# A linear-attention block with a gated feed-forward layer: the last block's output projection by seven half-size products, and a new order of issue

## The chip, the cores and the metric

The kernel runs on one core of a Trainium2 chip. A core has five engines that run side by side, each through its own queue in order: TensorE (PE, matmuls into the eight PSUM banks), VectorE (DVE), ScalarE (ACT), GpSimd (POOL) and SyncE (SP). Here GpSimd also issues the loads from HBM, and SyncE the stores and the transposes that run as transfers. The metric is the device time of one execution in microseconds (us), lower is better.

## The reference

The first stage is attention with projected keys and values. For each of 8 batches and 8 heads, with a sequence of 1024 and a head size of 64:

```python
k_proj = np.einsum('ks,bhsd->bhkd', E, k)          # 1024 rows -> 64
v_proj = np.einsum('ks,bhsd->bhkd', F, v)
scores = scale * np.matmul(q, k_proj.transpose(0, 1, 3, 2))
scores = scores - np.max(scores, axis=-1, keepdims=True)
attn = np.exp(scores)
attn = attn / (np.sum(attn, axis=-1, keepdims=True) + 1e-09)
attn_out = np.matmul(attn, v_proj)
```

The heads are put side by side, which gives x of 8192 x 512, and the second stage is a gated layer with a hidden width of 1536:

```python
gate = 1.0 / (1.0 + np.exp(-(x @ w_gate)))
val = x @ w_val
out = gate * val @ w_out
```

## The kernel before

Tokens are worked through in 16 blocks of 512, two blocks to a batch. A block goes through the gate and value products, a tanh on ScalarE, the hidden product `hT` on VectorE (1536 x 512, bf16, hidden units on partitions), and the output projection with `w_out` into `ost`, which is stored in four pieces of 256 KB (`store`, L1253). The attention of batch b+2 and b+1 is worked on while the blocks of batch b are multiplied.

*Seven products for eight.* The gate and value products (`seven`, L1108) and the output projections of blocks 1 to 14 (`o_jobs`, L1324) cut both matrices into 2 x 2 quarters and form the result from seven products of quarters, with sums of quarters made ahead by VectorE or GpSimd. For an output projection the quarters of `hT` are tokens by hidden units: `s_sum` (L1206) makes S1 = A21 + A22, S2 = S1 - A11, then, in the place of A21, A11 - A21, and, in the place of A12, A12 - S2 (S4). The sums of the weights are made once, into `wT` (`o_sum`, L1193). One product of quarters is two half-products of six matmuls of 256 columns (`o_product`, L1222). Three PSUM banks take part: a chain of products accumulates in one, ScalarE copies snapshots of it out (`snap`), and VectorE joins them with another bank (`merge`, L1355) or ScalarE copies a quarter out (`leave`, L1348). The product A12 x B21 reads A12 before S4 overwrites it, and the last product, A12 x B22, reads S4.

*Plain.* Blocks 0 and 15 go through `o_plain` (L1264) instead, since `o0p=1` and `o3p=1` in the table `AT` (L30):

```python
if AT[f"o{0 if not blk else 3 if blk == 2 * B - 1 else 2 - blk % 2}p"] > 0:
    return o_plain(blk, pos, step)
```

For block 15 that is three pieces of 128 tokens of 12 matmuls of 512 columns each, and the last piece in two halves of 12 matmuls of 256 columns. Each piece is copied out by ScalarE and stored by itself. In the issue order the piece of tokens 0 to 127 is last.

*The loads.* K and V of one batch come in two halves of 512 KB each (`load_kv`, L561; R is the half), q likewise (`load_q`, L582), all issued by GpSimd in its own order. K's buffer also serves as the place where the attention's result waits to be transposed into x (`turn_x`, L1709), so a half of K can be loaded only when the transposes of two token groups of the batch before have read it. `kv` (L1449) projects K and V in 16 matmuls of 512 columns and waits for all four halves. `transpose_q` (L1435) turns two heads of q at a time, four transfers for a batch, on SyncE's queue; the first waits for its half of q, and all that stands behind it on this queue waits with it. `turn_kd` (L1478) turns the projected K, and the scores (`score_pair`, L1622) wait for it and for q.

*The order.* A planner outside the kernel has written the order down. Each piece of work is a job with a number, in the order in which the code makes the jobs; `ORDER` (L159) lists the numbers in the order in which they are issued, each on its engine, and `PLACES` (L314) the PSUM bank or buffer of each tile that a job uses. A negative number in `ORDER` is a fill: idle matmuls of 256 columns times its size (`busy`, L724), so -2 is one of 512 columns. `Scheduler.run` (L359) reads both:

```python
for s, p in zip(slots, PLACES):
    s.at = p
return [(lambda i=i: fill(-i)) if i < 0 else self.jobs[i].body for i in ORDER]
```

Waits follow from the data (`Plan.add`), through semaphores, and an engine waits in `run` (L121) before the instruction that needs it. The constants of time in `AT` and `FB` set nothing any more, except the switches among them.

The numbers that matter below, for batch 2: 415 and 416 load the halves of K, 417 and 418 those of V, 419 loads the half of q that transposes 421 and 422 need and 420 the other, 421 to 424 are the four transposes of q, 425 is the projection, 428 turns the projected K, 581, 589, 597 and 605 are the scores.

Of the kernel before, what the change touches and what calls it, by code (L numbers as in the profile page):

```python
# [29 lines left out]
    s2=0, s3=0, s4=0, s5=0, s6=0, s7=0, o0p=1, o1p=0, o2p=0, o3p=1, x1=0, x2=0, x3=0, x4=1, g1=0, g2=0, g3=0,  # L30
# [123 lines left out]
class Job:  # L154
# [5 lines left out]
    16, -2, -2, -2, 17, 18, 0, 19, -2, -2, -2, -1, 30, 20, 4, 28, 21, 29, 5, 31, 1, -2, -2, -2, -2, -2, -2, 38,  # L160
    32, 22, 8, 33, 23, 39, 2, 34, 50, 24, 3, 48, 51, 40, 25, 35, -2, 26, 41, 36, 27, 42, 49, 37, -2, -2, -2, -2,
    -2, -2, -2, -1, 58, 52, 59, 68, 53, 43, 60, 61, -2, -1, 54, 69, 6, 55, 62, 44, 70, 46, 7, 75, 45, 47, 56,
    76, 9, 71, 72, 63, 10, 73, 57, -2, -2, 66, 13, 74, 77, -2, -1, 64, 14, 67, 140, 65, 78, 146, 12, 79, 134,
    194, 80, 81, 135, 128, 141, 195, 129, 130, 142, 197, 132, 136, 131, 138, 196, 143, 133, 144, 148, 137, 145,
    11, 84, 82, 188, 85, 147, 83, 149, 139, 15, 86, 104, 87, 102, 201, 105, 92, 152, 93, 103, 150, 88, 199, 164,
    94, 89, 106, 160, 362, 90, 156, 107, 162, 91, 95, 151, 112, 157, 154, 185, 96, 168, 108, 97, 172, 113, 109,
    184, 166, 114, 180, 158, 187, 110, 115, 100, 161, 101, 116, 111, 182, 98, 173, 174, 99, 170, 159, 122, 117,
    169, 175, 123, 163, 124, 200, 118, 120, 119, 181, 121, 171, 198, 125, 183, 218, 126, 234, 127, 186, 219,
    282, 202, 235, 165, 189, 190, 283, 210, 191, 220, 212, 222, 203, 221, 250, 167, 223, 238, 204, 251, 236,
    192, 239, 286, 193, 205, 224, 237, 225, 411, 254, 226, 241, 252, 207, 242, 206, 229, 227, 287, 245, 230,  # L170
    412, 240, 253, 284, 243, 153, 255, 228, 246, 298, 208, 257, 299, 209, 289, 155, 285, 231, 244, 258, 247,
    266, 232, 300, 248, 233, 261, 211, 267, 176, 249, 290, 270, 413, 262, 256, 178, 314, 301, 326, 271, 213,
    259, 273, 328, 272, 414, 274, 177, 315, 217, 329, 275, 302, 316, 260, 268, 216, 179, 263, 317, 327, 293,
    276, 318, 277, 294, 264, 319, 278, 279, 265, 439, 214, 303, 215, 320, 280, 269, 420, 281, 330, 547, 440,
    346, 338, 334, 442, 331, 335, 332, 336, 549, 333, 304, 342, 443, 337, 321, 339, 343, 305, 441, 322, 350,
    445, 306, 347, 323, 344, 340, 324, 348, 341, 351, 349, 309, 345, 307, 325, 363, 288, 352, 364, 354, 310,
    446, 311, 353, 355, 365, 370, 448, 291, 366, 444, 371, 358, 372, 447, 292, 356, 373, 359, 357, 375, 382,
    308, 367, 360, 295, 376, 553, 368, 548, 361, 377, 383, 369, 384, 387, 554, 449, 550, 385, 296, 374, 391,
    379, 555, 565, 388, 378, 380, 297, 381, 562, 389, 312, 386, 563, 552, 313, 394, 399, 564, 566, 392, 450,
    400, 395, 551, 556, 396, 401, 393, 397, 403, 567, 404, 419, 568, 390, 406, 557, 569, 407, 405, 408, 515,  # L180
    402, 431, 398, 467, 516, 531, 561, 451, 432, 517, 532, 433, 434, 571, 518, 533, 452, 572, 409, 534, 455,
    418, 573, 410, 453, 468, 560, 535, 456, 519, 454, 457, 415, 458, 520, 469, 417, 459, 522, 536, 460, 471,
    558, 523, 521, 570, 461, 538, 470, 559, 462, 577, 526, 423, 524, 463, 464, 539, 483, 527, 422, 528, 484,
    542, 489, 472, 543, 421, 485, 465, 474, 537, 529, 475, 424, 487, 416, 540, 473, 488, 478, 435, 578, 490,
    436, 544, 476, 438, 491, 499, 545, 525, 494, 486, 492, 480, 495, 574, 437, 481, 530, 496, 466, 681, 546,
    500, 575, 482, 493, 697, 479, 501, 698, 576, 503, 505, 497, 504, 701, 477, 682, 506, 702, 541, 745, 507,
    683, 502, 685, 508, 510, 686, 425, 778, 684, 511, 746, 509, 498, 777, 512, 426, 780, 687, 513, 688, 427,
    779, 704, 689, 699, 514, 428, 705, 747, 690, 692, 708, 700, 580, 693, 703, 579, 429, 709, 761, 694, 748,
    706, 783, 430, 781, 666, 710, 762, 695, 784, 664, 711, 763, 785, 782, 581, 691, 764, 749, 786, 582, 750,
    585, 787, 696, 583, 765, 791, 790, 752, 712, 584, 597, 586, 753, 789, 589, 792, 766, 590, 587, 768, 593,  # L190
    788, 756, 588, 769, 591, 793, 757, 598, 713, 794, 594, 751, 592, 797, 601, 595, 772, 599, 714, 596, 798,
    602, 600, 715, 754, 603, 717, 773, 716, 620, 617, 604, 758, 718, 618, 621, 707, 729, 622, 767, 799, 619,
    623, 605, 755, 759, 720, 665, 606, 613, 801, 721, 614, 609, 730, 802, 615, 607, 733, 803, 616, 770, 625,
    724, 734, 626, 731, 771, 725, 624, 774, 627, 610, 629, 736, 608, 628, 630, 632, 732, 760, 795, 611, 633,
    796, 775, 634, 612, 737, 644, 735, 635, 800, 637, 719, 631, 740, 638, 645, 636, 722, 639, 917, 738, 640,
    723, 641, 726, 642, 667, 918, 643, 727, 742, 656, 670, 804, 743, 728, 646, 805, 657, 744, 658, 919, 649,
    879, 776, 815, 650, 806, 651, 920, 816, 677, 921, 809, 679, 880, 810, 678, 817, 808, 741, 680, 883, 819,
    884, 653, 647, 885, 820, 654, 886, 818, 659, 822, 648, 887, 881, 652, 823, 888, 821, 882, 669, 890, 655,
    925, 892, 824, 891, 895, 660, 893, 831, 896, 828, 739, 832, 847, 829, 807, 825, 899, 668, 833, 900, 835,
    834, 848, 902, 836, 897, 903, 851, 898, 894, 838, 811, 826, 852, 912, 863, 911, 827, 854, 864, 812, 849,  # L200
    914, 814, 906, 850, 853, 907, 855, 867, 889, 662, 901, 856, 839, 1045, 904, 924, 860, 868, 858, 861, 842,
    663, 913, 870, 1046, 908, 843, 923, 1047, 909, 871, 1049, 1061, 922, 859, 910, 926, 905, 1062, 927, 661,
    1048, 869, 813, 1050, 915, 1063, 830, 874, 862, 1064, 837, 857, 1065, 916, 875, 929, 928, 840, 865, 931,
    866, 844, 872, 932, 873, 1052, 933, 876, 841, 1053, 1051, 845, 1066, 930, 877, 1056, 1141, 1068, 671, 1054,
    1069, 934, 1055, 846, 878, 1067, 672, 1058, 1070, 1109, 673, 1142, 1072, 1059, 1057, 938, 674, 1143, 1060,
    1074, 1146, 1110, 935, 1075, 936, 1073, 1125, 1144, 937, 1111, 1071, 1126, 939, 1145, 1112, 1127, 675, 940,
    1113, 1076, 1147, 676, 944, 942, 1128, 945, 1114, 943, 953, 949, 1148, 946, 1116, 1149, 950, 1129, 1117,
    1150, 947, 1130, 1120, 957, 948, 1132, 954, 951, 1151, 1121, 958, 952, 1156, 1155, 1153, 955, 961, 959, 969,
    1133, 965, 1157, 1152, 956, 962, 1136, 1158, 960, 970, 1077, 1161, 966, 1078, 1162, 963, 941, 967, 1081,
    973, 964, 1079, 971, 1163, 984, 968, 1131, 1080, 1137, 1165, 1082, 985, 974, 981, 986, 996, 1084, 972, 997,  # L210
    982, 989, 998, 1166, 983, 975, 999, 990, 993, 991, 1115, 976, 994, 1167, 987, 1093, 995, 1085, 977, 1118,
    992, 1083, 1094, 1088, 978, 1086, 979, 1001, 1154, 1122, 1000, 1134, 1008, 1095, 1123, 980, 1138, 1009,
    1097, 1002, 1096, 1003, 1159, 988, 1124, 1139, 1160, 1098, 1010, 1090, 1164, 1013, 1011, 1017, 1020, 1100,
    1018, 1091, 1004, 1168, 1101, 1014, 1140, 1169, 1015, 1029, 1019, 1089, 1104, 1027, 1041, 1092, 1005, 1021,
    1243, 1105, 1119, 1099, 1022, 1042, 1179, 1244, 1043, 1044, 1195, 1006, 1180, 1007, 1247, 1102, 1245, 1248,
    1016, 1183, 1170, 1181, 1184, 1023, 1250, 1174, 1182, 1106, 1012, 1196, 1249, 1107, 1246, 1186, 1024, 1197,
    1251, 1199, 1087, 1252, 1259, 1187, 1032, 1108, 1185, 1200, 1256, 1260, 1190, 1257, 1172, 1202, 1191, 1173,
    1135, 1254, 1203, 1211, 1103, 1255, 1261, 1188, 1212, 1206, 1263, 1207, 1281, 1264, 1276, 1213, 1198, 1192,
    1026, 1265, 1193, 1227, 1030, 1175, 1266, 1262, 1215, 1025, 1267, 1409, 1228, 1268, 1270, 1028, 1216, 1282,
# [1655 lines left out]
```

## Time and profile before

| | us |
|---|---|
| median of three executions | 518.62 (518.52, 518.62, 525.71) |
| the profiled execution | 523.59 |
| its span, first to last instruction | 521.6 |
| TensorE busy | 511.5 |
| VectorE busy | 433.9 |
| ScalarE busy | 371.9 |
| GpSimd busy | 171.2 |

A line of the timeline gives the start, the time taken, the engine, the line of the kernel, the operation with its output and inputs, how many instructions are joined in it, and in brackets the idle time before it and what ended that. In the stretches each engine has its busy time with the number of its instructions, and the last three figures are the clock granted to TensorE as a share of full speed, the share of the transfer engines and GB/s. A line of a queue (SPq) spans from the start of its first issue to the end of its last. "To landing" counts from a transfer's issue to its end. L516 is the helper through which all matmuls go, L530 that of ScalarE's copies, L545 that of sums, L1102 a plus, L1171 a hidden product, L557 a load, L1438 a transpose of q, L1481 that of the projected K, L1257 a store; PSUM banks are pF and pA.

### The profile page before, as it was taken

Reading aid. Unit: us, or ns where it says so; the run is one execution under the profiler, and the core shown is the slowest. Engines: PE = TensorE matmul, PEld = TensorE weight load, DVE = VectorE, ACT = ScalarE, POOL = GpSimd, SP = SyncE. Lnnn points to the kernel's source line nnn. Section 1 sums busy time; section 2 is a strip of 40 time slices with the busy share of each in tenths; the row PEclk is TensorE's granted clock in tenths of the full one; section 3 lists DMA queues with packets and bytes.
Section 4 is the critical chain, followed back from the end, with each engine's and each line's share of the span. In section 5 each row is a group of like instructions: output and inputs, shape, how many; then the busy total and the mean of one; then the engine's idle time right before and its main releaser. Section 6 shows DMA issues by size and latency. Waiting matters only on the chain.

```text
span 521.6 us, 12583 instructions
## 1 busy us (share of the span) xinstructions
PE 511.5 (98%) x4954; PEld 419.6 (80%) x4954; DVE 433.9 (83%) x847; ACT 371.9 (71%) x714; POOL 171.2 (33%) x200
## 2 busy tenths in 40 slices
PE   7999999979999999999999999999999999999997
PEld 4556757868898888888888888988898878888884
DVE  5779998496978999789987898989978799849880
ACT  1557866876978687876977778786887679676751
POOL 9894004601343114250263313440153400350020
PEclk9999999998999999999999999999999999999999
DMA  9999979996797536996999899981679923452004
GB/s 154 197 198 207 192 113 161 170 145 143 129 178 129 94 102 123 164 192 131 152 164 206 116 164 173 181 144 21 163 123 186 178 64 82 82 122 80 4 1 161
DMA packets 140554, 71.59 MB, mean 137 GB/s; under 512 B 97232, under 2 KB 132304, under 8 KB 140496
## 3 DMA queue, kind: packets, MB, share of 16 engines
q1 hardware_dynamic: 104560, 40.91, 39.8%
q0 software_dynamic: 35936, 29.89, 38.7%
q8 instruction: 39, 0.64, 0.5%
q14 instruction: 19, 0.16, 0.1%
HBM read 60.29 MB, written 16.78 MB: 148 GB/s over the span
## 4 chain that ended last, share of the span: by engine, by line
PE 97%; issue 1%; ACT 1%; DVE 0%; ACTq 0%
PE pA L516 50%; PE pF L516 48%; ACT ost L530 0%; ACT KVs L530 0%; ACT EFT L530 0%; ACT pA L530 0%; DVE warm L644 0%; DVE tV L645 0%; ACTq L129 0%
## 5 line engine op out<-in xcount | busy, mean ns | idle before, releaser
L530 ACT ACTIVATE spare<-pF 128x512 f32<-128x512 f32 (+2 forms) x169 | 93.3, 567 | 34.9 <-PE pF L516 20.6
L530 ACT ACTIVATE spare<-pA 128x512 f32<-128x512 f32 (+1 forms) x152 | 86.7, 585 | 32.8 <-PE pA L516 25.3
L545 POOL TENSOR_TENSOR hT<-hT,hS 128x512 bf16<-128x512 bf16 x42 | 48.1, 1159 | 129.1 <-PE pA L516 80.5
L1696 POOL TENSOR_TENSOR KVs<-spare,inv 128x384 bf16<-128x384 f32 (+1 forms) x52 | 37.1, 728 | 79.3 <-ACT spare L530 30.2
L1102 DVE TENSOR_TENSOR spare<-pA,spare 128x512 f32<-128x512 f32 x62 | 41.9, 684 | 8.2 <-ACT spare L530 3.4
L1171 DVE SCALAR_TENSOR_TENSOR hT<-spare,pF 128x512 bf16<-128x512 f32 x63 | 42.7, 680 | 6.1 <-PE pF L516 3.5
L516 PE MATMUL pF<-wO,hT 128*128 128x256 bf16 (+1 forms) x300 | 46.3, 298 | 0.0
L530 ACT ACTIVATE spare<-spare 128x512 f32<-128x512 f32 x74 | 45.3, 630 | 1.4 <-DVE spare L1102 1.2
L516 PE MATMUL pA<-wO,hT 128*128 128x256 bf16 (+1 forms) x312 | 41.8, 277 | 0.0
L1171 DVE SCALAR_TENSOR_TENSOR hT<-spare,pA 128x512 bf16<-128x512 f32 x53 | 35.7, 679 | 6.2 <-PE pA L516 4.4
L516 PE MATMUL pF<-xT,wV 128*128 128x256 bf16 (+1 forms) x240 | 39.3, 287 | 0.0
L516 PEld LDWEIGHTS pF<-wO,hT 128*128 128x128 bf16 x300 | 28.9, 98 | 10.2 <-ACT pF L530 0.4
L1102 DVE TENSOR_TENSOR spare<-pF,spare 128x512 f32<-128x512 f32 x48 | 32.7, 683 | 3.4 <-PE pF L516 2.4
L516 PE MATMUL pA<-xT,wG 128*128 128x256 bf16 (+1 forms) x208 | 33.5, 283 | 0.6 <-issue 0.6
L516 PEld LDWEIGHTS pA<-wO,hT 128*128 128x128 bf16 x312 | 30.1, 98 | 4.9
L516 PE MATMUL pF<-xS,tV 128*128 128x256 bf16 x224 | 33.5, 273 | 0.0
L557 POOL DMA_DIRECT2D Qb<-in_q_dram x18 | 14.0, 778 | 57.6 <-ACT kpD L530 21.6
L516 PE MATMUL pF<-xT,wG 128*128 128x256 bf16 (+1 forms) x200 | 32.8, 287 | 0.0
L516 PE MATMUL pA<-xS,wV 128*128 128x256 bf16 x216 | 32.0, 273 | 0.0
L516 PE MATMUL pA<-wT,hT 128*128 128x256 bf16 x240 | 31.6, 273 | 0.0
L516 PE MATMUL pA<-xS,tG 128*128 128x256 bf16 x208 | 30.6, 273 | 0.0
L516 PEld LDWEIGHTS pF<-xT,wV 128*128 128x128 bf16 x240 | 23.1, 98 | 6.0 <-ACT pF L530 0.5
(188 smaller groups left out, 1284.8 us busy)
## 6 DMA issues: line engine op xcount, KB each, us to landing
out_dram<-ost SPq DMA_DIRECT2D x63, 256.0 KB, 2.5
KVs<-in_v_dram POOLq DMA_DIRECT2D x15, 512.0 KB, 7.7
KVs<-in_k_dram POOLq DMA_DIRECT2D x14, 512.0 KB, 9.5
Qb<-in_q_dram POOLq DMA_DIRECT2D x14, 512.0 KB, 7.6
wO<-in_moe_w_out_dram POOLq DMA_DIRECT2D x1, 1536.0 KB, 16.0
KVs<-in_k_dram POOLq DMA_DIRECT2D x4, 256.0 KB, 7.2
Qb<-in_q_dram POOLq DMA_DIRECT2D x4, 256.0 KB, 9.8
wG<-in_moe_w_gate_dram POOLq DMA_DIRECT2D x4, 256.0 KB, 11.7
```

Of the source, the lines that this page charges most:

```text
L516: lambda e: e.matmul(o, lhsT, rhs, **kw),
L530: lambda e: e.activation(o, i, func, scale=scale),
L545: fn = lambda e: e.tensor_tensor(o, a, b, op)
L557: add("POOL", lambda e: e.dma_start(o, i), r=r, w=w, dma=sem, cost=0.78, nbytes=nbytes)
L1102: lambda e: e.tensor_tensor(PB(b)[:, :] if stay else BF(s), PB(b)[:, :], BF(s), ALU.add),
L1171: lambda e: e.scalar_tensor_tensor(o, y.rearrange("p (j c) -> p j c", j=2), 1.0, x.rearrange("p (j c) -> p j c", j=2), ALU.add, ALU.mult,),
L1696: fn = lambda e: e.tensor_tensor(xto.rearrange("p (g h d) -> p h g d", g=2, h=H)[:, hh[0] : hh[1], :, :], o[:, :, 0:DH].rearrange("p (h g) ...
```

## The change

`o3p` becomes 0, so block 15 goes through `o_jobs` like blocks 1 to 14: sums 1, 2 and 3 (a piece of four and a piece of two hidden tiles each) and sum 4 (in one piece) on VectorE, seven products of two halves, a copy, two snapshots and two copies out on ScalarE, two merges on VectorE, and four stores, of which those of tokens 0 to 255 wait for the last merge. It has 32 jobs (2879 to 2910) where the plain one had 15 (2879 to 2893); jobs 0 to 2878 are the same.

`ORDER` and `PLACES` are replaced as a whole. `ORDER` has 2911 jobs and 28 fills (25 of 512 columns, 3 of 256) where it had 2894 and 28 (24 and 4). The loads of batch 2 stand in the order 418, 415, 416, 419, 417 (it was 419, 418, 415, 417, 416), and three of the four transposes of q stand shortly ahead of the projection and one just behind it, where all four stood among the loads. In other batches loads and transposes of q have moved too.

```diff
-    s2=0, s3=0, s4=0, s5=0, s6=0, s7=0, o0p=1, o1p=0, o2p=0, o3p=1, x1=0, x2=0, x3=0, x4=1, g1=0, g2=0, g3=0,
+    s2=0, s3=0, s4=0, s5=0, s6=0, s7=0, o0p=1, o1p=0, o2p=0, o3p=0, x1=0, x2=0, x3=0, x4=1, g1=0, g2=0, g3=0,
 ORDER = (
...
-    418, 573, 410, 453, 468, 560, 535, 456, 519, 454, 457, 415, 458, 520, 469, 417, 459, 522, 536, 460, 471,
-    558, 523, 521, 570, 461, 538, 470, 559, 462, 577, 526, 423, 524, 463, 464, 539, 483, 527, 422, 528, 484,
-    542, 489, 472, 543, 421, 485, 465, 474, 537, 529, 475, 424, 487, 416, 540, 473, 488, 478, 435, 578, 490,
-    436, 544, 476, 438, 491, 499, 545, 525, 494, 486, 492, 480, 495, 574, 437, 481, 530, 496, 466, 681, 546,
-    500, 575, 482, 493, 697, 479, 501, 698, 576, 503, 505, 497, 504, 701, 477, 682, 506, 702, 541, 745, 507,
-    683, 502, 685, 508, 510, 686, 425, 778, 684, 511, 746, 509, 498, 777, 512, 426, 780, 687, 513, 688, 427,
...
-    2882, 2892, 2886, 2893, 2877, 2890, 2887, 2879, 2883, 2884, 2880, 2881,
...
+    468, 560, 519, 410, 456, 471, 454, 469, 418, 520, 533, 472, 522, 558, 534, 458, 470, 483, 459, 415, 457,
+    536, 462, 559, 460, 523, 521, 463, 538, 524, 464, 416, 539, 526, 465, 484, 419, 528, 527, 542, 417, 487,
+    543, 474, 488, 435, 537, 475, 529, 489, 473, 540, 530, 490, 525, 476, 544, 461, 570, 478, 499, 479, 485,
+    545, 480, 500, 574, 491, 481, 486, 501, 492, 494, 466, 436, 681, 495, 482, 438, 496, 503, 546, 697, 497,
+    504, 505, 682, 541, 506, 422, 575, 437, 507, 502, 685, 698, 508, 510, 424, 686, 745, 576, 498, 701, 477,
+    688, 423, 702, 512, 778, 689, 511, 683, 493, 425, 421, 782, 746, 513, 684, 514, 509, 749, 426, 692, 777,
...
+    2876, 2893, 2874, 2895, 2884, 2894, 2877, 2883, 2888, 2878, 2897, 2898, 2896, 2899, 2889, 2900, 2901, 2890,
+    2902, 2904, 2903, 2905, 2891, 2908, 2907, 2906, 2909, 2910,
 )
```

Of the last rows: 2881 and 2882 are the two pieces of sum 2, 2883 and 2884 those of sum 3, 2890 is sum 4; 2888 and 2889 are A12 x B21, 2892 and 2893 S2 x T2, 2895 and 2896 S1 x T1, 2897 and 2898 A21 x T3, 2901 and 2902 A22 x T4, 2904 and 2905 A12 x B22; 2900 and 2906 are the merges, 2907 to 2910 the stores.

345 rows, old and new, of tables (ORDER, PLACES) are left out of this document.

## The prediction

> **What bounds the kernel now.** I read the page first (span and busy time by engine), then the waits of TensorE, then the stretches around the longest of them, then the transfers that this wait hangs on.
>
> ```profile
> span 521.6 us, 12583 instructions
> PE 511.5 (98%) x4954; PEld 419.6 (80%) x4954; DVE 433.9 (83%) x847; ACT 371.9 (71%) x714; POOL 171.2 (33%) x200
> ...
> PE pA L516 <- issue: 3.8, 2, 3.2
> PE pF L516 <- issue: 1.4, 1, 1.4
> PE pA L516 <- DVE tV L645: 1.1, 1, 1.1
> ```
>
> TensorE is busy for 511.5 of 521.6 us. A busy share says little alone, since the ends of matmuls are modelled; the waits say more: the three longest are 3.2, 1.4 and 1.1 us, the last two before 7 us of the span, and nothing else in the body reaches 1 us. So the time is the matmul work itself, plus a head, a tail and one hole.
>
> ```profile
> 109.00:114.00 5.00, 4.79 (x44) 3.96 (x42) 5.00 (x10) 3.97 (x9) 0.00 (x0) 1.00 1.43 110
> 114.00:117.00 3.00, 0.01 (x1) 0.04 (x1) 2.23 (x5) 1.59 (x3) 0.00 (x0) 0.97 1.31 149
> 117.00:121.00 4.00, 4.00 (x21) 2.54 (x22) 0.00 (x0) 0.42 (x1) 0.00 (x0) 0.59 0.62 162
> 121.00:126.00 5.00, 5.00 (x48) 4.47 (x47) 4.64 (x8) 3.97 (x8) 0.71 (x1) 1.00 0.55 157
> ...
> 116.99 3.56 PE L516 MATMUL pA<-KVs,EFT 128*64 128x512 bf16 x16 [3.20 <-issue]
> ...
> 294.73 1.92 PE L516 MATMUL pA<-KVs,EFT 128*64 128x512 bf16 x16
> ```
>
> In the stretches (PE busy is the second figure, the granted clock the third from the end) the hole is 113.79 to 116.99 us. Behind it the granted clock is 0.59 for 4 us, and the projection that waited takes 3.56 us where the same 16 matmuls of batch 5 take 1.92. The hole thus costs 3.20 + 1.64 = 4.8 us, some 5 with the matmul after it.
>
> What came last there is the second half of batch 2's K:
>
> ```profile
> 99.63 17.21 SPq L1438 DMA_TRANSPOSE qT<-Qb  x4
> ...
> 103.49 0.78 POOL L557 DMA_DIRECT2D KVs<-in_k_dram x1 [4.60 <-DMA xT<-KVs]
> ...
> L557 POOL DMA_DIRECT2D KVs<-in_k_dram x1: 782/782/782, 103.5 to 103.5; - x1
> ...
> DMA to landing us min/median/max: 13.4/13.4/13.4
> ...
> L1438 SPq DMA_TRANSPOSE qT<-Qb x4: 1414/3978/7607, 99.6 to 112.8; - x4
> ...
> DMA to landing us min/median/max: 6.1/11.2/15.9
> ```
>
> GpSimd held this load 4.6 us for the transposes of x, issued it at 103.5, and it took 13.4 us to land, to 116.9, where the projection starts. Four transposes of q ran in the same time.
>
> The profiled execution took 523.59 us; the three timed ones 518.52, 518.62 and 525.71. 523.59 less the hole's 5.0 is 518.6, the median. I take it that the two short ones ran without this hole: **the median holds no such loss to win back.**
>
> **The change, part by part.** *Last block, output projection.* Now it is 3 x 12 full-width and 2 x 12 half-width matmuls.
>
> ```profile
> 128.52 1.31 PE pF L516 x12
> ...
> 513.28 2.59 PE pF L516 x12
> ```
>
> A half-width matmul is 1.31/12 = 0.109 us, a full-width one 2.59/12 = 0.216. Before: 3 x 2.59 + 2 x 1.31 = 10.39 us. After: seven products of two halves of six, 84 matmuls, 7 x 1.31 = 9.17. That is -1.22. The list has 25 and 3 idle fills of full and half width where it had 24 and 4: +0.216 - 0.109 = +0.11. All other TensorE jobs are the same, in another order. TensorE's work: **-1.11 us**.
>
> *The sums that the seven products need* run on VectorE.
>
> ```profile
> 495.40 0.68 DVE L545 TENSOR_TENSOR hT<-hT 128x1024 bf16<-128x1024 bf16 x1
> ...
> 496.60 0.41 DVE L545 TENSOR_TENSOR hT<-hT 128x512 bf16<-128x512 bf16 x1
> ...
> 508.82 0.68 DVE L1171 SCALAR_TENSOR_TENSOR hT<-spare,pA 128x512 bf16<-128x512 f32 x1
> ```
>
> Sums 1, 2 and 3 are a piece of 1024 and one of 512 each, 1.09 us; sum 4 is one piece of 1536, by the step between the rows 0.68 + 0.27 = 0.95; two merges like the row at 508.82 add 1.36. Together 5.6 us. In the trace VectorE has nothing after 509.5 while TensorE works to 518.5, 9 us, so the room is there. Where it could be late: sum 2 stands ahead of the last value product's plus, and TensorE wants it two half-products (1.3 us) behind that product; then come plus, hidden, a merge and sum 3, 3.1 us, and sum 3 is wanted five half-products later. Sum 4 cannot start before both halves of A12 x B21, which still read A12, and TensorE has four halves of A22 x T4 and A12 x B22 behind it, of which two (1.31 us) stand before the product that needs the sum. 0.95 us and the merge's 0.68 ahead of it (which waits for a snap) make 1.2 to 1.6 against 1.31: a wait of 0 to 0.4. Bounds 0 and 1; I take 0.1.
>
> *The end.* Now one ScalarE copy and one store of 256 KB follow the last matmul; after, a VectorE merge and two stores.
>
> ```profile
> 518.56 0.60 ACT L530 ACTIVATE ost<-pA 128x512 f32<-128x512 f32 x1 [1.97 <-PE pA L516]
> ...
> L1257 SPq DMA_DIRECT2D out_dram<-ost x1: 332/332/332, 519.2 to 519.2; - x1
> ...
> DMA to landing us min/median/max: 2.0/2.0/2.0
> ...
> L1257 SPq DMA_DIRECT2D out_dram<-ost x3: 332/432/466, 509.0 to 509.8; - x3
> ...
> DMA to landing us min/median/max: 2.0/2.3/2.4
> ...
> L1257 SPq DMA_DIRECT2D out_dram<-ost x3: 429/463/570, 272.3 to 273.4; - x3
> ...
> DMA to landing us min/median/max: 2.9/3.1/3.6
> ```
>
> The merge is 0.08 longer than the copy; the second store is issued 0.43 later; and with the other two stores just ahead of these it lands in 2.3 (the three at 509) rather than 2.0, at worst 3.6 (the three at 272, beside loads). So +0.8, bounds +0.5 and +2.1. I take the row at 509, since no load runs at the end.
>
> *The new order: loads and transposes.* I counted the matmuls that either list puts between two jobs and priced them by the rows above. Batch 2: the second K half (job 416) stood 88 half-width matmuls, 9.6 us, ahead of the projection (425); now 128, 14.0 us, and the last of the four loads (417) 116, 12.7 us. The four q transposes (421 to 424) stood 92 to 124 matmuls ahead; now 34, 20, 8 and one behind, after the loads. The last load to its projection, batches 2 to 7, before: 9.6, 7.9, 13.8, 17.5, 13.3, 11.1 us; after: 12.7, 10.7, 10.5, 11.8, 13.1, 17.3. So the two shortest leads grow, two in the middle shrink. What five loads in a burst take, batch 5 shows:
>
> ```profile
> 273.77 0.81 POOL L557 DMA_DIRECT2D KVs<-in_v_dram  x1
> 274.80 1.48 POOL L557 DMA_DIRECT2D KVs<-in_k_dram  x2 [0.22 <-issue]
> 276.26 0.76 POOL L557 DMA_DIRECT2D Qb<-in_q_dram  x1
> 277.00 0.77 POOL L557 DMA_DIRECT2D KVs<-in_v_dram  x1
> ...
> DMA to landing us min/median/max: 12.2/13.2/14.1
> ...
> 288.50 3.96 SPq L1438 DMA_TRANSPOSE qT<-Qb  x3
> ...
> 121.82 1.23 SPq L1481 DMA_TRANSPOSE kpD<-kpd  x1
> ...
> qT<-Qb SPq DMA_TRANSPOSE x28, 3.9
> ...
> kpD<-kpd SPq DMA_TRANSPOSE x6, 3.1
> ```
>
> The last two (q, then V) landed 12.2 and 14.1 us after their issue: the whole burst took 17.3 us, three stores in it. After, batch 2's burst begins 17.9 us ahead of its projection, batch 5's 18.3. Both fit, with 1 us or less to spare. In the median run I cost this at 0: the loads hide it as they do now, and if that cover goes the price is the rival's below. In an execution like the profiled one it is worth up to -5.0.
>
> The q transposes lose cover: the last of them stood 18.8, 28.2, 11.4, 14.2, 32.8 and 25.8 us ahead of the first scores, now 6.1, 29.0, 8.5, 11.8, 8.5 and 9.0. Behind each on SP's queue wait kpD's transpose, which the scores need, and the stores. A row of 3.9 fits into 6.1, so 0 again, but with the chain below as a rival.
>
> **The sum.** -1.11 + 0.1 + 0.8 = -0.2 us in the median: 518.6 becomes 518.4. The profiled execution, 523.59, less 5.0 and 0.2 is the same 518.4, if the hole does not come back.
>
> **Rivals.** *Slower: the transposes are now the late ones.* SP cannot issue the first until its half of q has landed; then four issues of 1.32 (3.96/3), one of 1.23 and kpD's landing, 3.1, make 9.6 us. From the q load to the first scores the new list leaves 21.4 us in batch 2, 19.0 in 4 and 18.6 in 6, so the scores wait once q takes over 11.8, 9.4 or 9.0 us. For it: 12.2 in the burst. Against: the page's 7.6 for 14 such loads, below, and that only batch 2's q is in a burst of five. At 13.4, what the K half took, they wait 1.6 and 4.0 in two places; with the clock falling behind a long hole 4.8 are lost as above. Time: 518.4 + 1.6 to 4.8 = 520 to 523.2. Chance 0.25. The Trainium skill (TensorE: Matmul & The Clock Gate, Part 1) says that the clock falls to half after an idle window of about 3.4 us. By that rule the wait of 1.6 costs no clock and the one of 4.0 does; the trace shows 0.59 behind 3.20 us idle.
>
> ```profile
> Qb<-in_q_dram POOLq DMA_DIRECT2D x14, 512.0 KB, 7.6
> ```
>
> The Trainium skill (DMA: Bandwidth & Descriptors, Queues, rings and completion order) says that each DMA engine takes turns between the queues it has work for, a packet at a time. By that rule the moved transposes still share with whatever load is left, and this rival would be the likelier one; that the K half took 13.4 us beside them agrees.
>
> *The change does not do what it says:* loads and transposes meet as before, and a projection waits (batch 5's last lead falls from 17.5 to 11.8, where such a load took 14.1: 2.3 us). Time 518.4 + 2.3 = 520.7; chance 0.12.
>
> *Faster: the tail costs nothing,* because the early copies let the first two stores drain and the timed runs held a little of the hole: the 1.11 stays whole, 517.5, or 516.5 with a further 1 us of small waits gone. Chance 0.18.
>
> **How the numbers follow.** The forecast, 518.4, has 0.45, its own range 517.5 to 519.9 by the bounds of the tail and of sum 4. Eight in ten: from 516.8, in the faster case, to 522.0, inside the first rival. 2% is 10.4 us, about what a measurement of this kernel can tell from no change; of the cases above only the first rival with two or three holes at once reaches it, 0.03, and the gain's whole ceiling, 1.11 in the median, is a tenth of it. Faster 0.01, same 0.96, slower 0.03.
>
> **What would show it.** After: no hole before the projection of batch 2 and a granted clock of 1.00 there; 84 half-width matmuls at the end in 9.2 us with under 0.5 us idle; two last stores that land some 3.4 us after the last matmul ends. Wrong, if TensorE waits over 1 us ahead of a projection or of the scores, or the end waits for sum 4.

## The result, and the profile after

The changed kernel takes **517.71 us** (median of 20 runs, 517.31 to 520.12). The kernel before, 20 runs beside it, takes 523.0 (518.52 to 527.06). The ratio of the means is 0.991, with a 95% interval of 0.989 to 0.994: 0.9% faster, inside the 2% that counts as no change. It leaves out the longest run before (527.06), which counts as slow. The profiled execution took 517.57 us. The forecast was 518.4, range 516.8 to 522.0, so the time after came out 0.7 us under the forecast, but against a time before that was 4.4 us over the one I started from. The two kernels differ most in their spread: 19 of the 20 runs after lie between 517.3 and 518.1, while of the 20 before seven lie under 520 and twelve over 521.9.

The page and the waits of TensorE, after (total, times, longest):

```profile
span 515.6 us, 12673 instructions
...
PE 509.4 (99%) x4975; PEld 420.6 (82%) x4978; DVE 443.7 (86%) x856; ACT 371.5 (72%) x714; POOL 173.2 (34%) x200
...
PE pA L518 <- DVE tV L647: 1.1, 1, 1.1
PE pF L518 <- ACT EFT L532: 0.3, 1, 0.3
PE pF L518 <- ACT spare L532: 0.2, 1, 0.2
```

Nothing is left but the start (1.1 and 0.3 us) and 0.2. The same stretches as before (span, PE busy, ..., granted clock third from the end), and the projection of batch 2 in the timeline of TensorE:

```profile
109.00:114.00 5.00, 5.00 (x47) 4.00 (x46) 5.00 (x10) 4.59 (x10) 0.00 (x0) 1.00 1.15 196
114.00:117.00 3.00, 3.00 (x29) 2.06 (x26) 2.86 (x6) 2.37 (x5) 0.00 (x0) 1.00 1.46 138
117.00:121.00 4.00, 4.00 (x39) 3.60 (x37) 3.41 (x7) 3.49 (x8) 0.95 (x2) 1.00 0.96 287
...
113.37 1.92 PE L518 MATMUL pF<-KVs,EFT 128*64 128x512 bf16 x16
```

The hole is gone, the clock stays at 1.00 and the 16 matmuls take 1.92 us. The transfers behind it: GpSimd's timeline, the landing of the K half, that of the last two loads (q, then V), SyncE's timeline, and the landing of the q transposes.

```profile
98.17 0.78 POOL L559 DMA_DIRECT2D KVs<-in_k_dram  x1
98.95 0.75 POOL L559 DMA_DIRECT2D Qb<-in_q_dram  x1
99.69 0.76 POOL L559 DMA_DIRECT2D KVs<-in_v_dram  x1
...
DMA to landing us min/median/max: 9.1/9.1/9.1
...
DMA to landing us min/median/max: 10.9/11.8/12.8
...
109.86 6.03 SPq L1440 DMA_TRANSPOSE qT<-Qb  x4
...
DMA to landing us min/median/max: 3.7/4.1/4.9
```

K goes out at 98.17 instead of 103.49, with no wait, and lands in 9.1 us instead of 13.4: at 107.3, where it was 116.9. The transposes begin only when the q half has landed, at 109.86 (98.95 + 10.9), when the burst is almost over, and land in a median of 4.1 us where it was 11.2. The last V half lands at 112.5 (99.69 + 12.8), 0.9 us ahead of the projection. The end, in TensorE's and VectorE's timelines and by the landing of the last two stores:

```profile
510.09 1.47 PE L518 MATMUL pA<-wO,hT 128*128 128x256 bf16 x12
...
508.43 0.69 DVE L1361 SCALAR_TENSOR_TENSOR ost<-pA,spare 128x512 f32<-128x512 f32 x1 [2.33 <-PE pA L518]
509.06 0.96 DVE L547 TENSOR_TENSOR hT<-hT,hS 128x1536 bf16<-128x1536 bf16 x1
511.70 0.69 DVE L1361 SCALAR_TENSOR_TENSOR ost<-pA,EF 128x512 f32<-128x512 f32 x1 [1.69 <-PE pA L518]
...
L1259 SPq DMA_DIRECT2D out_dram<-ost x2: 332/382/432, 512.5 to 512.8; - x2
...
DMA to landing us min/median/max: 2.1/2.2/2.3
```

TensorE's last matmul ends at 511.56 (510.09 + 1.47), so 4.0 us of the span lie behind it, where it was 3.1 (518.46 to 521.6): +0.9.

### The profile page after: what moved, and what is told of

It is laid out like the page before. It is cut to its first block, busy times and chain, and to the rows that moved or that the text cites. A ratio compares the mean times of both kernels' runs of the same rounds, so it can differ in the third digit from the quotient of the medians.

```text
span 515.6 us, 12673 instructions
## 1 busy us (share of the span) xinstructions
PE 509.4 (99%) x4975; PEld 420.6 (82%) x4978; DVE 443.7 (86%) x856; ACT 371.5 (72%) x714; POOL 173.2 (34%) x200
## 4 chain that ended last, share of the span: by engine, by line
PE 96%; DVE 3%; ACT 0%; issue 0%; DVEq 0%
PE pA L518 49%; PE pF L518 47%; DVE topf L1589 1%; DVE hT L1173 1%; DVE spare L1104 0%; DVE pF L1616 0%; DVE pA L1616 0%; DVE hT L547 0%; ACT spare L532 0%; DVE ost L1361 0%; DVE inv L1681 0%; ACT EFT L532 0%; ACT eT L532 0%; DVE KVs L1698 0%; DVE warm L646 0%
## 5 line engine op out<-in xcount | busy, mean ns | idle before, releaser
L532 ACT ACTIVATE spare<-pF 128x512 f32<-128x512 f32 (+2 forms) x157 | 87.4, 574 | 34.9 <-PE pF L518 23.4
L532 ACT ACTIVATE spare<-pA 128x512 f32<-128x512 f32 (+2 forms) x160 | 90.8, 583 | 26.7 <-PE pA L518 18.1
L1698 POOL TENSOR_TENSOR KVs<-spare,inv 128x256 bf16<-128x256 f32 (+1 forms) x48 | 34.7, 731 | 66.8 <-ACT spare L532 18.4
L1173 DVE SCALAR_TENSOR_TENSOR hT<-spare,pA 128x512 bf16<-128x512 f32 x65 | 43.7, 679 | 10.2 <-PE pF L518 6.1
L1104 DVE TENSOR_TENSOR spare<-pF,spare 128x512 f32<-128x512 f32 x57 | 38.5, 681 | 3.8 <-PE pF L518 2.1
L1173 DVE SCALAR_TENSOR_TENSOR hT<-spare,pF 128x512 bf16<-128x512 f32 x53 | 35.9, 679 | 4.9 <-PE pF L518 3.4
L518 PE MATMUL pA<-wO,hT 128*128 128x256 bf16 x264 | 34.4, 273 | 0.0
L518 PE MATMUL pA<-xT,wV 128*128 128x256 bf16 (+1 forms) x212 | 34.4, 285 | 0.0
L518 PE MATMUL pF<-xT,wV 128*128 128x256 bf16 (+1 forms) x196 | 32.1, 286 | 0.0
L547 POOL TENSOR_TENSOR xS<-xT,xS 128x512 bf16<-128x512 bf16 x14 | 16.9, 1207 | 32.5 <-DVE xS L547 27.5
```

Source lines behind the costliest of these rows:

```text
L518: lambda e: e.matmul(o, lhsT, rhs, **kw),
L532: lambda e: e.activation(o, i, func, scale=scale),
L547: fn = lambda e: e.tensor_tensor(o, a, b, op)
L1104: lambda e: e.tensor_tensor(PB(b)[:, :] if stay else BF(s), PB(b)[:, :], BF(s), ALU.add),
L1173: lambda e: e.scalar_tensor_tensor(o, y.rearrange("p (j c) -> p j c", j=2), 1.0, x.rearrange("p (j c) -> p j c", j=2), ALU.add, ALU.mult,),
L1698: fn = lambda e: e.tensor_tensor(xto.rearrange("p (g h d) -> p h g d", g=2, h=H)[:, hh[0] : hh[1], :, :], o[:, :, 0:DH].rearrange("p (h g) ...
```

## The experiments

The theory: the hole ahead of batch 2's projection comes from loads and transposes that run at the same time, and taking it away is most of the gain. Rival 1: K is simply issued too late, behind x's last transpose. Rival 2: the gain has another place. The edits move jobs in the written order with

```python
def put(order, moves):
    for i, at in moves:
        order = [j for j in order if j != i]
        order.insert(order.index(at), i)
    return tuple(order)
```

In batch 2, 415 to 418 are the K/V loads, 419 the q load, 421 to 424 the q transposes, 425 the projection. The kernel before ran beside each group of experiments: medians 523.45, 523.02 and 522.51 us.

**Back to the old places in the new order.**

```diff
 (after)
+ORDER = put(ORDER, ((419, 568), (423, 528), (422, 487), (421, 489), (424, 544)))
```

> The changed kernel, with batch 2's q load and its four q transposes moved back to the distances of the kernel before (226, and 92 to 124 half-size products ahead of the projection); everything else is the new order. Theory: the hole returns, 1 to 8 us from run to run, median 520 to 525 us. Rival 2 (it is something else in the new order): stays at 517.7 us.

Measured: 523.41 us (520.77 to 524.85, 12 runs). The waits of TensorE around batch 2, GpSimd's last load and its landing, then the transposes:

```profile
PE pF L528 <- DMA KVs<-in_v_dram: 2.5, 1, 2.5
...
99.40 0.75 POOL L569 DMA_DIRECT2D KVs<-in_v_dram  x1
...
DMA to landing us min/median/max: 14.6/15.8/17.0
...
L1450 SPq DMA_TRANSPOSE qT<-Qb x4: 1274/3385/9841, 95.1 to 108.6; - x4
...
DMA to landing us min/median/max: 10.6/13.7/18.1
```

Five jobs of one batch give the whole loss back. K is early here, and V, issued at 99.40 as in the changed kernel, is now what comes last: 17.0 us instead of 12.8, beside transposes that take up to 18.1. Rival 2 falls.

**Only the q load, in the old order.** The first attempt left one transpose ahead of the load that it should read (its quarter of batch 2's q is then the batch's before), which the text of the expectation does not say:

```diff
 (before)
+ORDER = put(ORDER, ((419, 528),))
```

> The kernel before, with nothing but batch 2's q load moved to where the new order has it, 124 instead of 226 half-size products ahead of the projection; the transposes keep their places in the list and start when q has landed. Theory (loads and transposes that run together slow each other): x's last transpose lands in about 4 us instead of 9.7, GpSimd does not wait for it, K is issued near 99.7 us instead of 103.5 and lands before 113.8; 518.3 to 519.3 us. Rival 1 (late issue of K) expects the same here, since the issue comes earlier: the two part on the run with the late transposes alone. Rival 2: near 523 us, as before.

Measured: 525.08 us (523.89 to 526.67). GpSimd's timeline:

```profile
108.78 0.78 POOL L567 DMA_DIRECT2D Qb<-in_q_dram  x1 [10.28 <-DMA qT<-Qb]
109.55 0.75 POOL L567 DMA_DIRECT2D KVs<-in_k_dram  x1
```

The load waited 10.28 us for that transpose, and K behind it in the queue. K then landed within 8 us, and the projection still waited 4.05 us for it, until 117.47. So an issue as late as 109.55 makes a hole by itself; of the theory the run tells nothing. With the load ahead of all four transposes:

```diff
 (before)
+ORDER = put(ORDER, ((419, 423),))
```

> The kernel before, with batch 2's q load moved behind two of the four K/V loads and ahead of all four q transposes in the list (the run before this one of the same kind had one transpose ahead of the load, and the load waited 10.3 us for it). Theory: x's last transpose lands in about 4 us instead of 9.7, K is issued near 99.7 us and lands ahead of 113.8; the transposes that need this q half start after 106; hole gone, 518.1 to 519.3 us. Rival (only the whole new order of batch 2 does it): a hole stays, 521 us or more.

Measured: 518.64 us (517.89 to 520.36, 12 runs), so -4.4 against the 523.02 beside it, from one load moved. GpSimd's timeline, and K's landing:

```profile
98.48 0.78 POOL L567 DMA_DIRECT2D Qb<-in_q_dram  x1
100.25 0.74 POOL L567 DMA_DIRECT2D KVs<-in_k_dram  x1 [0.99 <-DMA xT<-KVs]
...
DMA to landing us min/median/max: 13.1/13.1/13.1
```

The theory's chain held in its first half: x's last transpose lands in 6.8 us instead of 9.7, the wait for it falls from 4.60 to 0.99 us and K goes out 3.2 us earlier. The second half did not: K still takes 13.1 us, in the burst, and lands at 113.35, a tenth ahead of the projection at 113.47. So here the earlier issue alone took the hole away.

**Only the transposes.** Moved in the list alone:

```diff
 (before)
+ORDER = put(ORDER, ((422, 501), (424, 506), (423, 685), (421, 778)))
```

> The kernel before, with nothing but batch 2's four q transposes moved to where the new order has them, just ahead of the scores; its q load stays early. Theory (what makes the hole ahead of batch 2's projection is that the second K half lands beside the q transposes, 13.4 us instead of about 9): K is still issued near 103.5 us, lands near 112.6, ahead of the 113.8 us at which the projection can start; the hole is gone and the time is 518.3 to 519.3 us in nearly every run. Rival 1 (K is issued too late, because GpSimd waits 4.6 us for x's last transpose, and that is what counts): the hole stays, 521 to 524 us. Rival 2 (the time lost is not in this hole at all): a median near 523 us with the spread of the kernel before.

Measured: 519.29 us (517.99 to 526.62, 12 runs, five of them over 521). SyncE's timeline, K's landing and the projection, in an execution of 526.39:

```profile
100.25 19.39 SPq L1448 DMA_TRANSPOSE qT<-Qb  x4
...
DMA to landing us min/median/max: 14.6/14.6/14.6
...
119.65 3.73 PE L526 MATMUL pA<-KVs,EFT 128*64 128x512 bf16 x16 [5.71 <-issue]
```

A place in the list is no time: SyncE had nothing ahead of the transposes and began them at 100.25, as before at 99.63. The hole was 5.7 us in this execution. Why the others ran mostly without it I can't say; the list changes the order among the four and puts a store ahead of them. So a real wait, on K's landing:

```diff
 (before)
-        def transpose_q(r):
+        def transpose_q(r, late=()):
...
-                r=[("Q", hf, r // 2) for hf in range(2)],
+                r=[("Q", hf, r // 2) for hf in range(2)] + list(late),
...
-        turn_q(AT["tq2"])
+        turn_q(AT["tq2"], [("KV", 0, 1)])
+ORDER = put(ORDER, ((422, 501), (424, 506), (423, 685), (421, 778)))
```

(turn_q hands `late` on.)

> The kernel before, with batch 2's four q transposes made to wait until the second K half has landed (a real wait; moving them in the list alone had left their start at 100.3 us). The q load stays early. Theory (K lands late because the transposes of q run beside it): K is still issued near 103.5 us, because x's last transpose still lands late, but it lands in about 9 us, near 112.6; no hole of more than 0.5 us, 518.1 to 519.3 us in nearly every run. Rival 1 (the late issue of K, behind x's transpose that shares with the early q load, is enough): a hole stays, 520 to 524 us.

Measured: 519.25 us (517.91 to 520.27). GpSimd's timeline, K's landing, SyncE's timeline and the projection:

```profile
104.60 0.78 POOL L567 DMA_DIRECT2D KVs<-in_k_dram  x1 [5.73 <-DMA xT<-KVs]
...
DMA to landing us min/median/max: 8.8/8.8/8.8
...
113.49 5.71 SPq L1448 DMA_TRANSPOSE qT<-Qb  x4
...
113.69 1.92 PE L526 MATMUL pA<-KVs,EFT 128*64 128x512 bf16 x16
```

Rival 1 in its strict form, that the late issue is what makes the hole, falls: K goes out later than before (104.60) and still comes in time, since without the transposes beside it it lands in 8.8 us instead of 13.4. But the run with the q load moved shows that an earlier issue is enough too, with K as slow as before. What counts is the sum of issue and landing against the 113.8 us at which the projection could start. In the changed kernel both fell, the issue by 5.3 us and the landing by 4.3; which of the two it needed is not shown by itself.

**The kernel before, once more,** unchanged:

> The kernel before itself, for a second look at how its hole varies. Theory: with a time near 518.5 us, the second K half lands ahead of 113.8 us and there is no wait ahead of batch 2's projection; with a time over 521 us, a wait of 2 to 6 us stands there and the K half took over 11 us to land.

Measured: 524.01 us. K's landing, and the projection:

```profile
L557 POOL DMA_DIRECT2D KVs<-in_k_dram x1: 782/782/782, 102.8 to 102.8; - x1
...
DMA to landing us min/median/max: 14.4/14.4/14.4
...
117.27 2.88 PE L516 MATMUL pA<-KVs,EFT 128*64 128x512 bf16 x16 [3.59 <-issue]
```

The same hole, as expected of a time over 521. A short execution of the kernel before has not been profiled.

**The last block as before, in the new order.**

```diff
 (after; o3p=1)
+ORDER = tuple(i for i in ORDER if i < 2879) + (
+    2885, 2888, 2891, 2889, 2882, 2892, 2886, 2893, 2890, 2887, 2879, 2883, 2884, 2880, 2881)
+PLACES = PLACES[:-5] + (0, 2, 6, 5, 3)
```

> The changed kernel with the last block's output projection as before (3 x 12 full-width and 2 x 12 half-width matmuls, no sums, one store last), all of the new order up to there. The prediction's terms for the last block (-1.11 -0.0 for TensorE, +0.1 for the sums, +0.8 for the end) sum to -0.2, so 517.9 us. If the end costs nothing: 518.8 us. If the last block's projection brought nothing or a loss and all of the gain is in the order: 517.0 to 517.7 us.

Measured: 519.42 us (518.43 to 520.03, 12 runs). The waits of TensorE at the end:

```profile
PE pA L523 <- ACT EF L537: 0.7, 1, 0.7
```

Taking the interleaved half-products out let a product of the block before run into its snapshot: a wait of my own making. The profiled execution, 518.43, was the shortest of the twelve; what made the median 1.0 longer is not shown. With two jobs put in that gap:

```diff
+ORDER = [i for i in ORDER if i < 2879 and i not in (2810, 2872)]
+ORDER[ORDER.index(2869):ORDER.index(2869)] = [2810, 2872]
```

(and the tail appended as above)

> The changed kernel with the last block's output projection as before, and two TensorE jobs moved ahead of the product that waited 0.75 us for a snapshot in the first run of this kind. By the prediction's terms for the end (-1.11 for TensorE with the fills left as they are -1.22, +0.1 for the sums, +0.8 for the tail) this is 517.7 + 0.3 = 518.0 us. If the seven products are worth what the medians of the first run say less its wait, 518.7 us.

Measured: 517.88 us (517.66 to 518.38). The changed kernel, in other runs, has 517.71. So the seven products of the last block are worth some -0.2 us. The prediction's sum was -0.2 with the change of the fills, which this run keeps, and -0.3 without it. The traces agree term by term: from the start of batch 7's projection to TensorE's last end it takes 98.1 us in the changed kernel and 99.3 here, -1.2 as forecast without the fills, and the tail behind that end is 0.9 longer.

**The slower rival's price.** The q load behind GpSimd's next sum:

```diff
 (after)
+ORDER = put(ORDER, ((419, 503),))
```

> The changed kernel, with batch 2's q load moved back behind GpSimd's sum at 107.3 us, so that it is issued near 108.5 instead of 99.0. This prices the slower rival: q lands near 116 to 118 (6.6 to 9.1 us), four transposes of 1.3 us follow, kpD's transpose is issued near 121.5 to 123 and lands 3.1 later, so the scores, due at 121.4, wait 3.5 to 5 us, and the clock falls behind the wait: 521 to 524 us, by the rival's chain. If something else covers the scores: 517.7 us.

Measured: 520.19 us (519.86 to 521.28, 10 runs), +2.5. The waits of TensorE, the q load in GpSimd's timeline and its landing, SyncE's timeline, and the clock behind the longer wait:

```profile
PE pA L528 <- DMA eT<-KVs: 1.6, 1, 1.6
PE pA L528 <- DMA kpD<-kpd: 1.0, 1, 1.0
...
108.00 0.78 POOL L569 DMA_DIRECT2D Qb<-in_q_dram  x1
...
DMA to landing us min/median/max: 5.4/5.4/5.4
...
113.45 5.36 SPq L1450 DMA_TRANSPOSE qT<-Qb  x4
118.85 1.33 SPq L1493 DMA_TRANSPOSE kpD<-kpd  x1
...
133.00:136.00 3.00, 2.69 (x41) 2.26 (x42) 2.29 (x7) 1.63 (x4) 0.78 (x2) 1.00 0.72 131
```

The chain is the rival's: q, four transposes, kpD, scores. It is cheaper than I expected, as q, almost alone by then, landed in 5.4 us, and the scores waited 1.0; another 1.6 came up behind them, at the transposes of the exponentials. The clock stays at 1.00.

**An end in two banks,** to win the tail back. The last bank's product has each half in a bank of its own, so that the first half can be merged and stored while the second is computed:

```diff
 (after, in o_jobs)
+            last = blk == 2 * B - 1
+            f = [f, new_bank()] if last else [f, f]
...
-                job("DVE", pos + step * i + AT["dmerge"], body, name="mergeO")
+                for bank, js in ((f[0], (0,)), (f[1], (1,))) if last else ((f[0], (0, 1)),):
+                    job("DVE", pos + step * i + AT["dmerge"], lambda bank=bank, js=js: body(bank, js), name="mergeO")
```

> The changed kernel with the last block's last product in two banks, so that its first half is merged and stored while TensorE does the second half; the two merges of that bank become four of half the width. Behind the last matmul stand then 0.14 + 0.41 us for half a merge, one store issued 0.1 later and its landing of 2.0 to 2.3: 3.1 us instead of 4.0, so 516.8 us. If the landing of two stores at once, not the merge, sets the end: 517.3 to 517.7 us.

Measured: 517.38 us (516.80 to 518.25). VectorE's last merge, the stores and their landing:

```profile
511.07 0.42 DVE L1370 SCALAR_TENSOR_TENSOR ost<-pF,EF 128x256 f32<-128x256 f32 x1 [0.20 <-PE pF L523]
...
510.40 1.81 SPq L1264 DMA_DIRECT2D out_dram<-ost  x4
...
DMA to landing us min/median/max: 2.0/2.4/2.6
```

The merge behind the last matmul shrinks from 0.69 to 0.42 us, but four stores now go out one behind the other, the last at 511.8, and land in up to 2.6 instead of 2.3. Behind the last matmul (510.97) lie 3.8 us of 514.8, 0.2 less than in the changed kernel, not the 0.9 I reckoned. Two of the stores on ScalarE's queue:

```diff
-                "SP",
+                "ACT" if blk == 2 * B - 1 and tt > 1 else "SP",
```

> The kernel with the last product in two banks, and two of the last four stores issued by ScalarE instead of SyncE. In the run before, SyncE issued the four stores one behind the other from 510.4 to 512.2 us, the last merge having ended at 511.5. If that queue set the end, the last store goes out at 511.6 instead of 511.8 and shares with fewer: 0.2 to 0.5 less than 517.4, so 516.9 to 517.2 us. If the landing sets it: 517.4 us.

Measured: 517.76 us (516.97 to 518.92): no gain. In its profile the last store goes out at 512.3, as soon as the last merge ends, and lands in 2.9 us instead of 2.6: what the queue no longer costs, the landing takes. Neither version is told apart from the changed kernel by these runs.

## Why the prediction was right in its time, and wrong in its reason

**The hole: the step "the median holds no such loss to win back" failed.** The forecast of the change, -0.2, was 5 us off by it. The hole's mechanism, size and cure were right: the second K half beside the q transposes, some 5 us, gone after. But I put the median of three runs, 518.62, above the one execution that I could see into, 523.59. Those were four executions, two with the loss by their times; of the 20 runs beside the changed kernel twelve or more have it, by their times too. So the -5.0 that I kept for "an execution like the profiled one" belongs to the median: one load moved brings 523.02 to 518.64. That the time after was near all the same is no merit of this step: the long execution less its hole led to the same 518.4. And it was luck that the loss stayed inside the 2%, so that "no change" held.

**TensorE's work and the sums** (-1.11, +0.1): the waits show none for sum 4, which ends at 510.02, just ahead of the product that reads it, at 510.09. **The tail** (+0.8): measured +0.9. (The 3.4 us named among the signs does not fit this term, which on the 3.1 us before gives 3.9; 4.0 were measured.) Together -0.2 forecast, and -0.2 (517.88 to 517.71) measured. These terms held.

**A term left out.** Taking the old order's cured form at 518.64 and the new order with the old end at 517.88, another 0.8 us is in the order. A part of it can be named, in the kernel before's timeline of TensorE and, below it, in the waits of TensorE with the q load moved:

```profile
90.39 0.60 PE L516 MATMUL pA<-xT,wG 128*128 128x256 bf16 x4 [0.55 <-issue]
...
PE pF L526 <- issue: 2.2, 3, 1.1
```

The 0.55 is the second of the two waits in the row "issue: 3.8, 2, 3.2" that the prediction quotes; I used the 3.2 and let the 0.55 drop. All six profiles of the old order have it (0.5 to 0.6); of the seven of the new one six have none there, and that of the kernel put back has 0.16. What in the order removes it was not tried. The 1.1 stands ahead of batch 7's projection, in an execution of 519.58; its last load has 17.3 us to land in the new order and had 11.1, by the prediction's count, and no profile of the new order waits there, but none of the other five of the old one does either. The start varies by as much: in the first 14 us TensorE is idle for 2.2 to 3.0 us in the profiles of the old order and for 1.1 to 2.0 in those of the new one, with the first loads issued at the same times in the profiles of before and after. How the 0.8 is made up of these stays open.

**Loads and transposes at no cost in the median**: right after the change, with a margin of 0.9 us for the last V half where the prediction said 1 us or less.

**Rival 1** (transposes late) did not come about: they land in 4.1 us once they run behind the burst, and q lands in 10.9, inside the 11.8 that the prediction gave batch 2. It is real all the same: q issued 9.05 us later costs 2.5 us. The Trainium skill (DMA: Bandwidth & Descriptors, Queues, rings and completion order) has each DMA engine take turns between the queues it has work for; the 18.1 us of the kernel put back agree. It did not make this rival the likelier one here, as by 109.86 only the last V half was left to share with. **Rival 2** (batch 5's projection): no wait in the profile. **The faster rival** had the time, 517.5, and not the reason: its tail was to cost nothing, and it cost 0.9. Its other clause, small waits gone, came nearer: the 0.55 went.

## What to carry to other kernels

A hole that comes and goes from run to run shows as a spread of the times; with three runs and one profile, count the profiled one too, and take the loss for half present rather than absent. A transfer's duration is not its own: look at what else flies in that stretch, and hold back what is not needed yet by a data wait, since a later place in a list moves nothing when the queue is idle. Go through a row of waits wait by wait: the second one here was 0.55 us, and the forecast missed by 0.7.

## What the hardware showed that I had not expected

- The same four transposes land in 3.5 us (held back, and behind the burst) or in up to 18.1 beside loads, and the same K half in 8.8 or 14.6.
- What a hole cost by the clock was the same behind 2.49 and 3.59 us of idle time. In the kernel put back 2.49 us idle were followed by a lower clock, and in the second look at the kernel before 3.59 us idle (granted clock third from the end, first the one, then the other):

```profile
116.40:117.00 0.60, 0.56 (x4) 0.32 (x6) 0.60 (x3) 0.00 (x0) 0.00 (x0) 0.55 1.30 236
117.00:120.00 3.00, 3.00 (x16) 0.98 (x13) 1.03 (x2) 0.00 (x0) 0.00 (x0) 0.52 0.08 18
120.00:123.00 3.00, 3.00 (x29) 2.70 (x29) 0.64 (x2) 2.85 (x6) 0.00 (x0) 1.00 0.17 34
```

```profile
117.00:120.00 3.00, 2.73 (x16) 1.79 (x16) 0.00 (x0) 0.00 (x0) 0.00 (x0) 0.71 0.87 217
120.00:123.00 3.00, 3.00 (x21) 2.33 (x21) 1.84 (x3) 1.76 (x4) 0.00 (x0) 0.72 0.15 31
```

The clock lost is 0.6 x 0.45 + 3 x 0.48 = 1.7 us in the first and 3 x 0.29 + 3 x 0.28 = 1.7 us in the second. Behind the 3.20 us of the prediction's profile it is 4 x 0.41 = 1.6 us. In stretches of half a microsecond each of the three shows full clock, then 0.50 for some 3.4 us, then full clock; in the second the drop comes only 1 us into the projection, which therefore took 2.88 us and not 3.6. Behind the 5.71 us of the run with the transposes moved in the list it was more, some 2 us: the clock was half from 116.9, well ahead of the projection, until 123.6. Behind 1.64 us idle (the slower rival's run) and 1.12 us (batch 7, above) the clock stayed at 1.00.

The Trainium skill (TensorE: Matmul & The Clock Gate, Part 1) gives an idle window of about 3.4 us, free-running, for the clock to fall. The 1.64 us without loss agree; the 2.49 us with one are shorter than that.
